# A fourth weight buffer and a fourth PSUM bank in the expert stage of an attention and MoE kernel

## The chip, the cores and the metric

One Trainium2 chip; the program runs on one of its cores. The metric is the device time of one execution in microseconds (us), and lower is better.

## What is computed

Sliding-window attention, then a dense gated layer, then a layer of eight experts of which each token takes one:

```python
# q, k, v: [4, 8, 576, 64]
scores = where((rel >= 0) & (rel < 64), q @ k.T / 8, -1e9)
x = softmax(scores) @ v                     # as [2304, 512]
x = ((x @ w1) * (x @ w2)) @ w3 @ w_out      # [512, 1024] x 2, [1024, 1024], [1024, 512]
e = argmax(x @ w_gate)                      # one of 8 experts for each token
h = maximum(x[mask] @ ew1[e], 0)            # [512, 1024]
out[mask] = gate_w * sigmoid(x @ w_output_gate)[e] * (h @ ew2[e])   # [1024, 512]
```

The weights and tokens are float32. The number of tokens that go to each expert is known only when the program runs.

## The kernel before

Every float32 product is made in three passes (PASSES): each operand is split into a high half in a shorter format and a low half, the rest, and high x high, high x low and low x high are added up in PSUM. A weight therefore needs a split before it is used: ACT copies the high half (ehigh, line 676), DVE subtracts it from the raw chunk (elow, line 680).

Up to about 490 us attention and the dense layer run in an order that a planner writes out. After that comes the expert stage, with which the change deals. Its order is the program's on TensorE alone; on the other engines the framework's scheduler sets the order, and each engine and queue then works strictly in that order.

The expert stage goes through the experts e = 0 to 7. For each:

- static_block takes the first 256 tokens. The first layer makes hidden features in eight groups f of 128: 12 matmuls of 256 columns (line 924) into one PSUM bank, then the eviction by ACT (line 929, relu, the high half) and DVE (line 930, the low half) into hT. The banks come from ps_ab, tag "ab", which has three. The second layer (mm2, line 905) makes two blocks of 128 tokens: for each f three matmuls of 512 columns, which read hT of that f.
- row_block takes the next 128 tokens, if the expert has more than 256, with line 958 for the first layer; a fourth block and a loop for more follow inside branches. Its input xT is made by xT_block: four transposes (line 728), then a split (lines 421 and 422). The third block's tile is exT2 (two buffers), that of the fourth block and of the loop exT3. Its first half accumulates in the bank of ps_v, tag "pv".
- The hooks at1, at2 and at3 of static_block call esplit eight times: they split the weights of expert e + 1, eight chunks of 512 KB each (four of the first layer, four of the second). Chunks are numbered through all experts, 0 to 63; chunks 24 to 31 are expert 3's and are split in expert 2's block. The raw chunks are fetched by SP (eload, lines 662 and 664) into three buffers, tag ck2: after each split the load of the chunk three further on is asked for, and it has to wait until DVE has emptied its buffer.
- The rows of the next experts' tokens come by gathers that POOL issues (line 707) and the results go out by scatters (line 897). All of these share the DMA engines with the weights.

ex[0] is the memory pool of the later part of the stage; it is opened behind expert 0's static block, where the pools of the dense layer are closed, and lies in their memory. Expert 0's own block uses the dense layer's tiles for its hT.

Of the kernel before, what the change touches and what calls it, by code (L numbers as in the profile page):

```python
# [9 lines left out]
F32 = mybir.dt.float32  # L10
F32R = mybir.dt.float32r
# [10 lines left out]
NT, DM, DF, NE = B * S, H * D, 1024, 8  # L22
# [374 lines left out]
def attention_moe_moe_kernel(ctx: ExitStack, tc: tile.TileContext, q0, k0, v, w1, w2, w3, w_out,  # L397
# [4 lines left out]
    def pool(stack, name, **kw):  # L402
        return stack.enter_context(tc.tile_pool(name=name, bufs=kw.pop("bufs", 1), **kw))
# [8 lines left out]
    ps_ab = pool(ctx, "ps_ab", bufs=3, space=PSUM)  # L412
    ps_acc = pool(ctx, "ps_acc", bufs=2, space=PSUM)
    ps_s = pool(ctx, "ps_s", bufs=2, space=PSUM)
    ps_v = pool(ctx, "ps_v", space=PSUM)
# [212 lines left out]


    exp_state = {}  # L630

    def open_exp():
        s_att.close()
        exp_state["p"] = pool(s_exp, "exp", side="right")
# [13 lines left out]
    def eslot(e, i):  # L648
        if ew[e][i] is None:
            j = 0 if e % 2 == 0 else 2 + 2 * i  # L650
            ew[e][i] = [wslot(j), wslot(j + 1)]
        return ew[e][i]

    items = [(e, i, c) for e in range(NE) for i in range(2) for c in range(4)]
    nload, nsplit = [0], [0]

    def eload(to):
        while nload[0] < min(to, len(items)):
            e, i, c = items[nload[0]]
            t = exp_state["p"].tile([128, 1024], F32, name="ck2", tag="ck2", bufs=3)  # L660
            if i == 0:
                nc.sync.dma_start(out=t, in_=ew1[e, 128 * c:128 * c + 128, :])
            else:
                nc.sync.dma_start(out=t.rearrange("p (a d) -> p a d", a=2),
                                  in_=ew2[e, 256 * c:256 * c + 256, :].rearrange("(a p) d -> p a d", p=128))
            eq.append(t)
            nload[0] += 1
# [7 lines left out]
    def ehigh():  # L675
        nc.scalar.activation(out=eparts()[0], in_=eq[0], func=AF.Copy)  # L676

    def elow(low=V):
        hi, lo = eparts()
        low.tensor_tensor(lo, eq.popleft(), hi.bitcast(F32), op=ALU.subtract)  # L680
        nsplit[0] += 1

    def esplit(low=V):
        if nsplit[0] < len(items):
            ehigh()
            elow(low)
            eload(nsplit[0] + 3)

    def step(n=1):
        for _ in range(n):  # L690
# [4 lines left out]
    idx, xg, xTs = {}, {}, {}  # L695
# [35 lines left out]
    def xT_block(g, xT, c0):  # L731
        split(g_turn(g), xT[:, 0, :, c0:c0 + 128], xT[:, 1, :, c0:c0 + 128])
# [153 lines left out]
    post.extend(rt.parts(*GROUPS[NU - 1]))  # L886


    ex = [None]

    def y_tile():
        return ex[0].tile([128, DM], F32, name="y", tag="y", bufs=3)
# [1 line left out]
    def emit_out(ps, ix, j, own=y_tile):  # L894
        y = own()
        nc.scalar.activation(out=y, in_=ps, func=AF.Copy, scale=ix.bitcast(F32)[:, j, 1:2])  # L896
        nc.gpsimd.indirect_dma_start(out=out[:, :],  # L897
                                     out_offset=bass.IndirectOffsetOnAxis(ap=ix[:, j, 0:1], axis=0),
                                     in_=y, in_offset=None, bounds_check=NT - 1, oob_is_err=False)

    def mm2(hT, c0, w, hooks={}):
        ps = ps_acc.tile([128, 512], F32, name="yps", tag="acc")
        for f in range(8):
            for i, (a, b) in enumerate(PASSES):
                mm(ps, lhsT=hT[f][:, a, c0:c0 + 128], rhs=w[b][:, 512 * f:512 * f + 512],  # L905
                   start=f == 0 and i == 0, stop=f == 7 and i == 2)
            if f in hooks:
                hooks[f]()
        return ps

    def h_tile(f):
        return ex[0].tile([128, 2, 256], F32R, name="hT", tag="hT", bufs=8)

    def static_block(e, ix, at1, at2, at3, h_tile=h_tile, y_tile=y_tile):

        w1e = eslot(e, 0)
        xT = xTs.pop(e)
        hT = []
        for f in range(8):
            ps = ps_ab.tile([128, 512], F32, name="hps", tag="ab")  # L920
            for kk in range(4):
                c = 1024 * kk + 128 * f
                for i, (a, b) in enumerate(PASSES):
                    mm(ps[:, 0:256], lhsT=w1e[a][:, c:c + 128], rhs=xT[:, b, kk, :],  # L924
                       start=kk == 0 and i == 0, stop=kk == 3 and i == 2)
                if (f, kk) in at1:
                    at1[f, kk]()
            h = h_tile(f)
            nc.scalar.activation(out=h[:, 0, :], in_=ps[:, 0:256], func=AF.Relu)
            nc.vector.scalar_tensor_tensor(out=h[:, 1, :], in0=ps[:, 0:256], scalar=0.0,  # L930
                                           in1=h[:, 0, :].bitcast(F32), op0=ALU.max, op1=ALU.subtract)
            hT.append(h)
            if f in at1:
                at1[f]()
        w2e = eslot(e, 1)
        for j, at in enumerate((at2, at3)):
            ps = mm2(hT, 128 * j, w2e, at)
            emit_out(ps, ix, j, y_tile)

    def row_block(xT, ix, j, w1e, w2e):  # L940
        hs, hT = [], {}

        def turn(z):
            tp = ps_s.tile([128, 512], F32, name="tps2", tag="S")
            for f in range(4):
                nc.tensor.transpose(tp[:, 128 * f:128 * f + 128], hs[z][:, 128 * f:128 * f + 128], ident)
            tp = tp.rearrange("p (a b) -> p a b", a=4)
            for f in (0, 2):
                h2 = ex[0].tile([128, 2, 2, 128], F32R, name="h2", tag="hT", bufs=8)
                split(tp[:, f:f + 2, :], h2[:, 0], h2[:, 1])  # L950
                hT[4 * z + f], hT[4 * z + f + 1] = h2[:, :, 0, :], h2[:, :, 1, :]

        for z in range(2):
            ps = (ps_s if z else ps_v).tile([128, 512], F32, name="rps", tag="S" if z else "pv")
            for kk in range(4):
                c = 1024 * kk + 512 * z
                for i, (a, b) in enumerate(PASSES):
                    mm(ps, lhsT=xT[:, a, kk, 0:128], rhs=w1e[b][:, c:c + 512],
                       start=kk == 0 and i == 0, stop=kk == 3 and i == 2)
                if z and kk == 1:  # L960
                    turn(0)
            h = ex[0].tile([128, 512], F32, name="hs", tag="y", bufs=3)
            nc.scalar.activation(out=h, in_=ps, func=AF.Relu)
            hs.append(h)
        ps = mm2(hT, 0, w2e, {1: lambda: turn(1)})
        emit_out(ps, ix, j)

    def row_loop(lo, hi, w1e, w2e):

        with tc.For_i(lo, hi, 128) as r:  # L970
            ix = ex[0].tile([128, 1, 2], I32, name="ixd", tag="ixd", bufs=1)
            nc.sync.dma_start(out=ix[:, 0, :], in_=tab[bass.ds(r, 128), :])
            g = ex[0].tile([128, DM], F32, name="xgd", tag="y", bufs=3)
            nc.gpsimd.indirect_dma_start(out=g, out_offset=None, in_=x2d[:, :],
                                         in_offset=bass.IndirectOffsetOnAxis(ap=ix[:, 0, 0:1], axis=0))
            xT = ex[0].tile([128, 2, 4, 128], F32R, name="exT3", tag="exT3", bufs=1)
            xT_block(g, xT, 0)
            row_block(xT, ix, 0, w1e, w2e)

# [42 lines left out]
    w1e, w2e = eslot(0, 0), eslot(0, 1)  # L1022
    n0 = nc.values_load(rt.done[0:1, 0:1], min_val=0, max_val=256)
    n = nc.values_load(rt.cnt[0:1, 0:1], min_val=0, max_val=NT)
    xT = ex[0].tile([128, 2, 4, 128], F32R, name="exT2", tag="exT2", bufs=2)
# [4 lines left out]
    with tc.If(n > n0):  # L1030
        row_block(xT, idx[0], 0, w1e, w2e)
        with tc.If(n > n0 + 128):  # L1032
            row_loop(n0 + 128, n, w1e, w2e)
    for e in range(1, NE):
        at1 = {f: esplit for f in (0, 2, 4, 6)}
        at1[1] = turn
        at3 = {3: esplit, 6: esplit}
        if e + 1 < NE:
            rows(e + 1, tab[e * NT + NT:e * NT + NT + 512, :], 4)
            at3.update({0: lambda e=e: begin(e + 1), 2: turn, 5: turn})  # L1040
        static_block(e, idx[e], at1, {f: esplit for f in (1, 5)}, at3)
        w1e, w2e = eslot(e, 0), eslot(e, 1)
        n = nc.values_load(rt.cnt[0:1, e:e + 1], min_val=0, max_val=NT)  # L1043
        with tc.If(n > 256):  # L1044
            row_block(xTs.pop((e, 2)), idx[e], 2, w1e, w2e)
            with tc.If(n > 384):  # L1046
                xT = ex[0].tile([128, 2, 4, 128], F32R, name="exT3", tag="exT3", bufs=1)
                xT_block(xg[e, 3], xT, 0)
                row_block(xT, idx[e], 3, w1e, w2e)
                with tc.If(n > 512):  # L1050
                    row_loop(e * NT + 512, e * NT + n, w1e, w2e)
    order.close()
    s_ex2.close()
    s_exp.close()
# [46 lines left out]
```

## Time and profile before

| what | value |
|---|---|
| time, median of 3 runs | 799.07 us (795.09 to 799.41) |
| the profiled execution's own time | 800.18 us |
| its span, first to last instruction | 798.5 us |
| TensorE matmuls busy | 741.0 us, 93% of the span |
| DVE, ACT, POOL busy | 378.0, 303.8, 168.4 us |
| moved by DMA | 97.47 MB, mean 122 GB/s |

PE is TensorE, PEld its weight loads, DVE is VectorE, SPq and ACTq the queues of an engine's DMA and branch instructions. In a timeline a row is one instruction or several alike that follow each other: start, time from the first's start to the last's end, engine, line, what is written from what, shape, count, and in brackets how long the engine stood idle before it and what ended that. PEclk is TensorE's granted clock as a share of its full 2.4 GHz; 0.5 is 1.2 GHz. Variables that hold tiles carry the name that the trace gives them: raw chunks are ck, split weights w or wx, the first layer's banks hps, the second's yps.

### The profile page before, as it was taken

The numbers are of one execution on the slowest core, as the hardware profiler recorded it, in microseconds if no ns is written. First come the engines' busy times: TensorE is split into PE (matmuls) and PEld (weight loads), VectorE is DVE, ScalarE is ACT, GpSimd is POOL, SyncE is SP. The second block draws the span as 40 slices with busy tenths as digits, with TensorE's granted clock in tenths as the row PEclk, the third lists the DMA queues.
The fourth block names the chain that finished last, engine by engine and source line by source line (L and its number), as shares of the span: only waits on it lengthen the run. The fifth ranks groups of instructions, "written<-read, shape, count | busy, mean of one in ns | idle before, by whom it ended". The sixth has DMA issues, their size and how long they took to land. (4 is left out here: it accounts for less than half of the span.)

```text
span 798.5 us, 13578 instructions
## 1 busy us (share of the span) xinstructions
PE 741.0 (93%) x5227; PEld 661.0 (83%) x5227; DVE 378.0 (47%) x907; ACT 303.8 (38%) x683; POOL 168.4 (21%) x196
## 2 busy tenths in 40 slices
PE   3799979999999999999999998888989899899995
PEld 2577769989999999999999998868878778788874
DVE  6988995444445344344423226516264552462110
ACT  3554443433334233433221215425254544453221
POOL 6654552110111311110110010050213212010010
PEclk9999998999999999999999999989999999999998
DMA  8946662322222132015000004855456572650010
GB/s 324 409 170 221 208 215 76 122 82 77 98 77 102 33 103 77 8 32 173 27 4 26 28 14 167 185 136 179 126 184 209 187 236 71 228 181 26 6 40 13
DMA packets 38933, 97.47 MB, mean 122 GB/s; under 512 B 9747, under 2 KB 9875, under 8 KB 38848
## 3 DMA queue, kind: packets, MB, share of 16 engines
q1 hardware_dynamic: 33072, 83.06, 31.5%
q0 software_dynamic: 4816, 12.77, 5.1%
q8 instruction: 50, 0.82, 0.4%
q10 hardware_dynamic: 960, 0.53, 0.2%
q14 instruction: 35, 0.29, 0.1%
HBM read 86.83 MB, written 10.65 MB: 122 GB/s over the span
## 5 line engine op out<-in xcount | busy, mean ns | idle before, releaser
L560 PE MATMUL ab<-xt,w 128*128 128x256 f32 x1728 | 229.1, 287 | 0.5 <-DVE f L513 0.5
L560 PEld LDWEIGHTS ab<-xt,w 128*128 128x128 f32 x1728 | 219.1, 193 | 5.2 <-DVE f L513 0.8
L584 PE MATMUL acc<-w,gt 128*128 128x512 f32 x432 | 114.4, 399 | 3.4 <-ACT gt L572 2.6
L584 PEld LDWEIGHTS acc<-w,gt 128*128 128x128 f32 x432 | 76.1, 189 | 17.4 <-ACT gt L572 3.1
L568 DVE TENSOR_TENSOR a_sb<-ab,a_sb 128x256 f32<-128x256 f32 x72 | 30.5, 424 | 121.6 <-PE ab L560 113.2
L905 PE MATMUL yps<-w,hT 128*128 128x512 f32 x336 | 83.9, 401 | 0.0
L177 POOL TENSOR_TENSOR pp<-pp,r 128x384 f32<-128x384 f32 x48 | 39.7, 829 | 191.4 <-DVE r L172 131.5
L680 DVE TENSOR_TENSOR w<-ck,w 128x1024 fp32r<-128x1024 f32 x48 | 58.1, 1221 | 33.9 <-ACT w L676 25.3
L905 PEld LDWEIGHTS yps<-w,hT 128*128 128x128 f32 x336 | 62.4, 192 | 12.1
L572 ACT ACTIVATE gt<-a_sb 128x256 fp32r<-128x256 f32 x72 | 30.0, 416 | 99.8 <-DVE a_sb L568 95.2
L540 PE MATMUL wps<-w,w3T 128*128 128x512 f32 x192 | 52.5, 416 | 11.7 <-ACT w3T L527 11.5
L676 ACT ACTIVATE w<-ck 128x1024 fp32r<-128x1024 f32 x48 | 50.3, 1057 | 32.9 <-DMA ck<-in_moe_w 30.4
L897 POOL DMA_INDIRECT out<-y,idx x20 | 20.1, 1004 | 194.1 <-ACT y L896 139.7
L163 ACT ACTIVATE pp<-sps,nm 128x128 f32<-128x128 f32 x144 | 42.4, 369 | 39.1 <-DVE nm L154 36.8
L924 PE MATMUL hps<-exT,w 128*128 128x256 f32 x384 | 49.1, 286 | 8.0 <-DVE hT L930 6.0
L924 PEld LDWEIGHTS hps<-exT,w 128*128 128x128 f32 x384 | 46.8, 191 | 11.1 <-DVE hT L930 7.3
L540 PEld LDWEIGHTS wps<-w,w3T 128*128 128x128 f32 x192 | 35.4, 195 | 19.3 <-ACT w3T L527 11.5
L565 ACT ACTIVATE a_sb<-ab 128x256 f32<-128x256 f32 x72 | 27.8, 386 | 54.9 <-PE ab L560 51.7
L389 POOL DMA_INDIRECT tab<-ent,pos x18 | 17.7, 982 | 139.2 <-DVE pos L376 42.2
L576 DVE TENSOR_TENSOR gt<-a_sb,gt 128x256 fp32r<-128x256 f32 x72 | 31.3, 435 | 25.4 <-ACT gt L572 24.4
L422 DVE TENSOR_TENSOR exT<-gps,exT 128x512 fp32r<-128x512 f32 x23 | 15.9, 692 | 57.0 <-ACT exT L421 55.5
L924 PE MATMUL hps<-exT,wx 128*128 128x256 f32 x288 | 37.2, 286 | 5.8 <-DVE hT L930 4.3
(132 smaller groups left out, 1035.6 us busy)
## 6 DMA issues: line engine op xcount, KB each, us to landing
ck<-in_moe_w SPq DMA_DIRECT2D x88, 512.0 KB
q<-in_q SPq DMA_DIRECT2D x16, 576.0 KB
v<-in_v SPq DMA_DIRECT2D x16, 576.0 KB
k<-in_k SPq DMA_DIRECT2D x16, 320.0 KB
w<-in_moe_w_out SPq DMA_DIRECT2D x8, 512.0 KB
w<-in_moe_w SPq DMA_DIRECT2D x8, 512.0 KB
x2d<-x SPq DMA_DIRECT2D x16, 256.0 KB
x2d<-x ACTq DMA_DIRECT2D x2, 256.0 KB
```

Source lines behind the costliest of these rows:

```text
L163: nc.scalar.activation(out=p[:, o], in_=ps[:, o], func=AF.Exp, bias=nm[:, i:i + 1], scale=0.125)
L177: nc.gpsimd.tensor_tensor(p, p, s.pop(("r", g)).unsqueeze(2).to_broadcast([128, 3, 128]), op=ALU.mult)
L540: mm(ps, lhsT=t[:, a, 128 * j:128 * j + 128], rhs=wo[b][:, o:o + 512], start=g == 0 and j == 0 and x == 0, stop=g == 1 and j == 3 and x == 2)
L560: mm(ps, lhsT=w[a][:, c:c + 128], rhs=x[:, b, kk, :], start=kk == 0 and i == 0, stop=kk == 3 and i == 2)
L568: V.tensor_tensor(asb[u, m], gps.pop((u, m, 1)), asb[u, m], op=ALU.mult)
L572: nc.scalar.activation(out=g[:, 0, :], in_=asb[u, m], func=AF.Copy)
L576: V.tensor_tensor(g[:, 1, :], asb.pop((u, m)), g[:, 0, :].bitcast(F32), op=ALU.subtract)
L584: mm(accs[u][t], lhsT=g[:, a, 128 * t:128 * t + 128], rhs=ws["w34"][b][:, 512 * m:512 * m + 512], start=m == 0 and i == 0, stop=m == 7 and ...
L676: nc.scalar.activation(out=eparts()[0], in_=eq[0], func=AF.Copy)
L680: low.tensor_tensor(lo, eq.popleft(), hi.bitcast(F32), op=ALU.subtract)
L905: mm(ps, lhsT=hT[f][:, a, c0:c0 + 128], rhs=w[b][:, 512 * f:512 * f + 512], start=f == 0 and i == 0, stop=f == 7 and i == 2)
L924: mm(ps[:, 0:256], lhsT=w1e[a][:, c:c + 128], rhs=xT[:, b, kk, :], start=kk == 0 and i == 0, stop=kk == 3 and i == 2)
```

## The change

Three edits in the expert stage. From the opening of ex[0] on, raw chunks whose number leaves 3 when divided by 4 go to a new buffer, ck3, in that pool, and eload runs four chunks ahead instead of three. In static_block the groups f = 3 and f = 7 take the bank of ps_v, tag "pv", so that four banks go round. The tile exT3 is dropped: the fourth row block and the loop turn their rows into the third block's tile, and row_loop gets it as an argument.

```diff
--- before.py
+++ after.py
@@ -628,6 +628,7 @@
 
 
     exp_state = {}
+    ex = [None]
 
     def open_exp():
         s_att.close()
@@ -657,7 +658,10 @@
     def eload(to):
         while nload[0] < min(to, len(items)):
             e, i, c = items[nload[0]]
-            t = exp_state["p"].tile([128, 1024], F32, name="ck2", tag="ck2", bufs=3)
+            if ex[0] is not None and nload[0] % 4 == 3:
+                t = ex[0].tile([128, 1024], F32, name="ck3", tag="ck3", bufs=1)
+            else:
+                t = exp_state["p"].tile([128, 1024], F32, name="ck2", tag="ck2", bufs=3)
             if i == 0:
                 nc.sync.dma_start(out=t, in_=ew1[e, 128 * c:128 * c + 128, :])
             else:
@@ -684,7 +688,7 @@
         if nsplit[0] < len(items):
             ehigh()
             elow(low)
-            eload(nsplit[0] + 3)
+            eload(nsplit[0] + (3 if ex[0] is None else 4))
 
     def step(n=1):
         for _ in range(n):
@@ -886,7 +890,6 @@
     post.extend(rt.parts(*GROUPS[NU - 1]))
 
 
-    ex = [None]
 
     def y_tile():
         return ex[0].tile([128, DM], F32, name="y", tag="y", bufs=3)
@@ -917,7 +920,7 @@
         xT = xTs.pop(e)
         hT = []
         for f in range(8):
-            ps = ps_ab.tile([128, 512], F32, name="hps", tag="ab")
+            ps = (ps_v if f % 4 == 3 else ps_ab).tile([128, 512], F32, name="hps", tag="pv" if f % 4 == 3 else "ab")
             for kk in range(4):
                 c = 1024 * kk + 128 * f
                 for i, (a, b) in enumerate(PASSES):
@@ -965,7 +968,7 @@
         ps = mm2(hT, 0, w2e, {1: lambda: turn(1)})
         emit_out(ps, ix, j)
 
-    def row_loop(lo, hi, w1e, w2e):
+    def row_loop(lo, hi, w1e, w2e, xT):
 
         with tc.For_i(lo, hi, 128) as r:
             ix = ex[0].tile([128, 1, 2], I32, name="ixd", tag="ixd", bufs=1)
@@ -973,7 +976,6 @@
             g = ex[0].tile([128, DM], F32, name="xgd", tag="y", bufs=3)
             nc.gpsimd.indirect_dma_start(out=g, out_offset=None, in_=x2d[:, :],
                                          in_offset=bass.IndirectOffsetOnAxis(ap=ix[:, 0, 0:1], axis=0))
-            xT = ex[0].tile([128, 2, 4, 128], F32R, name="exT3", tag="exT3", bufs=1)
             xT_block(g, xT, 0)
             row_block(xT, ix, 0, w1e, w2e)
 
@@ -1030,7 +1032,7 @@
     with tc.If(n > n0):
         row_block(xT, idx[0], 0, w1e, w2e)
         with tc.If(n > n0 + 128):
-            row_loop(n0 + 128, n, w1e, w2e)
+            row_loop(n0 + 128, n, w1e, w2e, xT)
     for e in range(1, NE):
         at1 = {f: esplit for f in (0, 2, 4, 6)}
         at1[1] = turn
@@ -1042,13 +1044,13 @@
         w1e, w2e = eslot(e, 0), eslot(e, 1)
         n = nc.values_load(rt.cnt[0:1, e:e + 1], min_val=0, max_val=NT)
         with tc.If(n > 256):
-            row_block(xTs.pop((e, 2)), idx[e], 2, w1e, w2e)
+            xT = xTs.pop((e, 2))
+            row_block(xT, idx[e], 2, w1e, w2e)
             with tc.If(n > 384):
-                xT = ex[0].tile([128, 2, 4, 128], F32R, name="exT3", tag="exT3", bufs=1)
                 xT_block(xg[e, 3], xT, 0)
                 row_block(xT, idx[e], 3, w1e, w2e)
                 with tc.If(n > 512):
-                    row_loop(e * NT + 512, e * NT + n, w1e, w2e)
+                    row_loop(e * NT + 512, e * NT + n, w1e, w2e, xT)
     order.close()
     s_ex2.close()
     s_exp.close()
```

The scheduler also places instructions differently. On ACT, in expert 2's block before, from the second eviction on (L929 are the evictions hT in the order f1, f2 and so on, L676 the splits of chunks 26 to 31):

```order
L676 ACTIVATE w_6848<-ck_6507 128x1024
L929 ACTIVATE hT<-hps 128x256 x2
L676 ACTIVATE w_6848<-ck_6852 128x1024
L929 ACTIVATE hT<-hps 128x256
L676 ACTIVATE w_6985<-ck_6888 128x1024
L929 ACTIVATE hT<-hps 128x256 x2
L676 ACTIVATE w_6985<-ck_6924 128x1024
L929 ACTIVATE hT<-hps 128x256
L676 ACTIVATE w_6985<-ck_6960 128x1024
L929 ACTIVATE hT<-hps 128x256
L676 ACTIVATE w_6985<-ck_6989 128x1024
```

The same place after the change (now L932 and L680):

```order
L680 ACTIVATE w_6847<-ck_6488 128x1024
L932 ACTIVATE hT<-hps 128x256
L680 ACTIVATE w_6847<-ck_6508 128x1024
L932 ACTIVATE hT<-hps 128x256
L680 ACTIVATE w_6984<-ck_6851 128x1024
L932 ACTIVATE hT<-hps 128x256
L680 ACTIVATE w_6984<-ck_6887 128x1024
L932 ACTIVATE hT<-hps 128x256 x2
L680 ACTIVATE w_6984<-ck_6923 128x1024
L932 ACTIVATE hT<-hps 128x256
L680 ACTIVATE w_6984<-ck_6959 128x1024
L932 ACTIVATE hT<-hps 128x256
```

Both begin with chunk 26's split. Before, f3 stands behind the split of chunk 27, f4 and f5 behind 28, f6 behind 29 and f7 behind 30; after, f3 stands behind 28, f4 and f5 behind 29, f6 behind 30 and f7 behind 31. DVE's order follows, with the splits of 27 and 28 next to each other ahead of f3.

On SP, at the branch into expert 0's row blocks (L1030 before), the piece before that holds the first chunk load behind the branch, chunk 19:

```order
L970 UNCONDITIONAL_BRANCH
L1032 UNCONDITIONAL_BRANCH
L1030 UNCONDITIONAL_BRANCH
L662 DMA ck_6283<-in_moe_w 128x1024
L664 DMA ck_6326<-in_moe_w 128x2x512
```

After, with the same branch now at L1032:

```order
L1045 TENSOR_LOAD cnt
L1045 ISA x2
L666 DMA ck_6282<-in_moe_w 128x1024
L1032 COMPARE_AND_BRANCH
L1034 REGISTER_ALU
L1034 COMPARE_AND_BRANCH
```

Chunk 19's load, the first into ck3, has moved from behind the branch to ahead of it. In each later block one load has moved in the same way, from the start of the next expert's block to the end of this one's. TensorE's and POOL's orders are unchanged.

## Rows read from the trace of the kernel before

**Rows 1.** The page, part 1: busy us (share of the span) and instructions.
```profile
PE 741.0 (93%) x5227; PEld 661.0 (83%) x5227; DVE 378.0 (47%) x907; ACT 303.8 (38%) x683; POOL 168.4 (21%) x196
```

**Rows 2.** Windows of the first layers, experts 2 to 7: stretch, length, engines, PEclk, DMA, GB/s.
```profile
580.59:594.76 14.17, 12.30 (x97) 11.76 (x97) 9.21 (x13) 9.44 (x15) 2.34 (x2) 1.00 0.52 176
607.36:622.26 14.90, 12.35 (x97) 11.74 (x97) 9.21 (x13) 9.56 (x15) 2.53 (x2) 1.00 0.61 196
634.86:649.12 14.26, 12.36 (x96) 11.75 (x97) 9.21 (x13) 9.30 (x15) 2.74 (x2) 1.00 0.65 211
673.84:688.30 14.46, 12.31 (x97) 11.77 (x97) 9.20 (x13) 9.42 (x15) 1.98 (x2) 1.00 0.58 187
703.05:715.78 12.73, 11.99 (x96) 11.69 (x97) 9.20 (x13) 8.43 (x15) 1.02 (x1) 1.00 0.66 198
740.50:752.27 11.77, 11.76 (x96) 11.67 (x97) 2.97 (x7) 3.04 (x8) 0.98 (x1) 1.00 0.02 6
```

**Rows 3.** Timeline of TensorE, expert 1's first layer: start, length, what [idle before <-releaser].
```profile
554.34 1.69 PE L924 MATMUL hps<-exT,w 128*128 128x256 f32 x12 [1.38 <-DVE hT L930]
```

**Rows 4.** Waits, 480 us to the end: who, for whom: us in total, times, longest.
```profile
PE hps L924 <- DVE hT L930: 10.4, 9, 2.3
...
PE gps L728 <- DMA xg<-x2d,idx: 2.6, 3, 1.2
```

**Rows 5.** Timeline of TensorE, expert 2's block.
```profile
580.59 10.90 PE L924 MATMUL hps<-exT,wx 128*128 128x256 f32 x84 [0.43 <-PEq L1046]
593.22 1.70 PE L924 MATMUL hps<-exT,wx 128*128 128x256 f32 x12 [1.73 <-DVE hT L930]
594.76 6.31 PE L905 MATMUL yps<-w,hT 128*128 128x512 f32 x27
```

**Rows 6.** Timeline of ACT, expert 2's block.
```profile
587.10 1.06 ACT L676 ACTIVATE w<-ck 128x1024 fp32r<-128x1024 f32 x1 [1.51 <-DMA ck<-in_moe_w]
...
590.52 1.06 ACT L676 ACTIVATE w<-ck 128x1024 fp32r<-128x1024 f32 x1 [2.09 <-DMA ck<-in_moe_w]
...
593.62 1.06 ACT L676 ACTIVATE w<-ck 128x1024 fp32r<-128x1024 f32 x1 [0.28 <-DMA ck<-in_moe_w]
```

**Rows 7.** Timeline of DVE, expert 2's block.
```profile
588.19 1.23 DVE L680 TENSOR_TENSOR w<-ck,w 128x1024 fp32r<-128x1024 f32 x1 [1.34 <-ACT w L676]
589.33 0.42 DVE L930 SCALAR_TENSOR_TENSOR hT<-hps,hT 128x256 fp32r<-128x256 f32 x1
591.61 1.23 DVE L680 TENSOR_TENSOR w<-ck,w 128x1024 fp32r<-128x1024 f32 x1 [1.86 <-ACT w L676]
592.75 0.75 DVE L930 SCALAR_TENSOR_TENSOR hT<-hps,hT 128x256 fp32r<-128x256 f32 x2
```

**Rows 8.** Timeline of SP: the first chunk loads in the blocks of experts 1 and 2.
```profile
544.71 0.34 SPq L662 DMA_DIRECT2D ck<-in_moe_w  x1
...
583.60 0.33 SPq L662 DMA_DIRECT2D ck<-in_moe_w  x1
584.74 8.49 SPq L664 DMA_DIRECT2D ck<-in_moe_w  x4
```

**Rows 9.** Windows, columns as in rows 2: expert 2's loads, expert 0's gathers.
```profile
584.00:593.00 9.00, 7.35 (x58) 6.81 (x56) 5.79 (x9) 4.95 (x10) 1.34 (x1) 1.00 0.77 262
522.00:527.00 5.00, 2.40 (x12) 1.75 (x12) 1.13 (x2) 1.88 (x3) 3.22 (x4) 0.75 0.64 177
```

**Rows 10.** Windows, columns as in rows 2: the matmuls after expert 5's first layer.
```profile
688.30:696.22 7.92, 7.92 (x31) 6.32 (x30) 2.90 (x4) 2.09 (x3) 0.00 (x0) 0.78 0.74 249
```

**Rows 11.** Timeline of TensorE: expert 0's second layer, and the first transposes behind it.
```profile
510.97 11.07 PE L905 MATMUL yps<-w,xt 128*128 128x512 f32 x48
522.97 0.66 PE L728 MATMUL gps<-ident,xg 128*128 128x128 f32 x4 [0.93 <-DMA xg<-x2d,idx]
```

**Rows 12.** Timeline of TensorE: the transposes of expert 7's fourth block.
```profile
774.98 0.60 PE L728 MATMUL gps<-ident,xg 128*128 128x128 f32 x4
```

## The prediction

> **What bounds the kernel now.** I read the page first: TensorE is busy 741.0 of the 798.5 us [rows 1]. So time can come off only where TensorE has nothing to do, and the change touches the expert stage alone. There I cut out, with the windows view, each expert's first layer, from its first matmul of line 924 to its first of line 905 [rows 2]. Expert 7 splits no weights any more and takes 11.77 us: the price of the 96 matmuls alone, 1.47 us for each of the eight f. Experts 2 to 6 do the same in 14.17, 14.90, 14.26, 14.46 and 12.73 us, which is 2.40, 3.13, 2.49, 2.69 and 0.96 more. Expert 1 has four transposes among them, so I take the wait that its row shows, 1.38 [rows 3]. Together the six blocks lose **13.0 us**. The waits view names who ends most of it: DVE's eviction of hT, nine times, 10.4 us [rows 4].
>
> Why the eviction is late shows in expert 2's block, which starts at 580.59 [rows 5 to 8]. ACT and DVE work in order, and the evictions of f (lines 929, 930) stand between the splits of expert 3's chunks 24 to 31 (lines 676, 680). Three chunks are there at the start. Chunk 27 can be fetched only when DVE has emptied chunk 24's buffer: issued at 583.60, split by ACT at 587.10. Chunk 28, issued at 584.74, is split at 590.52, after ACT stood 2.09 us waiting for the DMA [rows 6, 8]. Behind it wait f4 and f5, and DVE is done with f4 at about 592.75 + 0.37 = 593.12 [rows 7]. With three banks f7 needs f4's, so TensorE starts it at 593.22 [rows 5], instead of 580.59 + 7 x 1.47 = 590.88.
>
> **The change, part by part.**
>
> *The bank.* f7 now needs f3's bank, not f4's. In expert 2's block f3 is free at 589.33 + 0.42 = 589.75 [rows 7], before 590.88: no stall is left. The second layer then starts at 580.59 + 11.77 = 592.36 and takes 0.70 us per f (27 matmuls, nine f, 6.31 us [rows 5]), so it wants f4 at 595.2 and f7 at 597.3; f4 is there at 593.1. The new bank, pv, is otherwise taken by the row blocks, which come after the block; nobody waits for it.
>
> *The fourth buffer.* It brings one chunk more into the idle stretch, but the built order uses that up: on ACT f3 now stands behind chunk 28, f4 and f5 behind 29, f7 behind 31. In expert 2's block chunk 28 goes out when chunk 24 is done, at 583.60, as chunk 27 did, and if it lands as that did, f3 is free at 589.75 and f4 at 593.1, both as before. DVE takes 27 and 28 before f3, but 27 is there from the start and is over before 28 comes. Chunk 31 is asked for after 27's split, not after 28's, which ended at 592.84 [rows 7]; if it lands by 593.62, when ACT could split chunk 30 before [rows 6], f7 is done at 593.62 + 1.06 + 1.23 + 0.42 = 596.3, before 597.3. So by this chain the bank carries the gain, and the buffer leaves four chunks to land inside the block instead of five. I count the **13.0 us** whole. The unknown is how long chunk 28 takes: 3.5 us from issue to split (583.60 to 587.10) or 5.8 (584.74 to 590.52) [rows 6, 8]. It is the first load after an idle stretch, as chunk 27 was, so I take 3.5 and keep 5.8 for the range.
>
> *The clock.* After expert 5's stall the 27 matmuls that follow took 7.92 us at a granted clock of 0.78 [rows 10], after expert 2's the same took 6.31 [rows 5]. Without the stall I expect 6.31 there: **1.6 us** off. Only one of the stalls was followed by a fall, so this term is 0 to 1.6.
>
> *The first load into the new buffer.* The order moves chunk 19's load from behind expert 0's branch to before it. Its memory was that of expert 0's last hT tiles, so it goes out when expert 0's second layer ends, at 510.97 + 11.07 = 522.04 [rows 11], and not at 544.71 [rows 8]. There it meets the gathers of line 707, for which TensorE waits three times, 2.6 us in all [rows 4, 11]. SP has only branches behind the load, so nothing is queued there. The loss is bounded by nothing, if the gathers keep their turn, and by 2.0 us, if they wait for all of it: 0.52 MB at the 262 GB/s of a busy stretch [rows 9]. The DMA is 0.64 busy in these 5 us, which leaves 0.36 x 5 = 1.8 us for the load, but not where it likes; I take the middle, **1.0 us** lost. The Trainium skill says (DMA: Bandwidth & Descriptors, section Queues, rings and completion order) that each DMA engine takes turns, packet by packet, between the queues that have work. By that the last of the three gathers would meet the whole load and come 2.0 us late, and the sum would be 787.6; no row here shows these gathers beside a load.
>
> *The rest.* Later row blocks now write into the third one's xT. Only expert 7 ran a fourth block here, and its transposes, at 774.98 [rows 12], stand on TensorE behind all the third block's matmuls: nothing is left to wait for. The new buffer is as large as the tile that goes, 4 KB a partition. Expert 0's block also gets the bank; its waits are for other things, so I count nothing.
>
> Sum, against the profiled execution's own 800.18 us: 800.18 - 13.0 - 1.6 + 1.0 = 786.6. That execution stands 1.1 us over the median of 799.07, less than the clock's term alone; I forecast **786.5 us**.
>
> **The rivals.**
>
> *The loads stay late.* If chunk 28 takes 5.8 us, it lands at 589.4; ACT and DVE then need 1.06 + 1.23 + 0.42, some 0.1 of it overlapped, until f3 is free at 592.0, and f7 starts 1.1 us late: about half of expert 2's 2.40 stays. Over six blocks 6.5 us are won and the clock's term is lost: 800.2 - 6.5 + 1.0 = 794.7. For it speaks that the DMA is 0.77 busy there [rows 9]; against it, the 3.5 us at the same place in the queue. Chance 0.15.
>
> *The bank does nothing.* Then only the buffer acts, and by the chain above f3 and f4 come free when they did: 800.2 + 1.0 = 801.2, which can't be told from no change. Against it: the row that ends the stall is f4's eviction, and f3's is 3.4 us earlier [rows 7]. Chance 0.07. A sentence of the Trainium skill reads that way, of a kernel whose matmuls wait for DMA: "Adding PSUM double-buffering gave no further gain" (TensorE: Matmul & The Clock Gate, section HAM oscillation). By it the sum would be 801.2 as well; the trace agrees that a DMA stands at the root, but shows a bank between it and TensorE.
>
> *Slower: the evictions behind one more split.* f3 was behind chunk 27 and is now behind 28. If 28 lands late enough, f7 starts later than before. To lose 4.0 us in all, with 1.0 from the gathers, the six blocks must lose 13.0 + 3.0 = 16.0, or 2.7 each: f3 free at 593.6, so chunk 28 landing at 591.0, 7.4 us after its issue, in every block. That gives 804.2. It decides from 6.9 us on, where f3 would come free when f4 did; the longer of the two rows is 5.8. Chance 0.03.
>
> **How the numbers follow.** A measurement of this kernel can tell about 0.5%, 4.0 us, from no change. The forecast has 0.75, with a range of its own of 783.5 to 789: the load costing 0 to 2.0, the clock giving 0 to 1.6, and the median's 1.1 under the profiled execution. To it come 0.15 for 794.7 (still faster, by just over 0.5%), 0.07 and 0.03. So faster 0.90, same 0.07, slower 0.03. The range runs from 783.5 to 795.0, through the second case, and leaves the last two out.
>
> **What would show it.** In the profile after, the windows of rows 2 should read 11.8 to 12.2 us for experts 2 to 6; TensorE's wait for DVE's hT should fall from 10.4 to under 2 us; ACT should still wait for chunks between f2 and f6; chunk 19's load should be issued near 522, and the waits for gathers grow from 2.6 to some 3.6 us. If the windows stay at 14, the bank is not the limit; if they read 13, chunk 28 lands late, and its issue and split tell by how much.

## The result, and the profile after

The changed kernel takes **785.77 us** (median of six executions, five of them from 785.29 to 786.65), against 798.97 us (795.09 to 803.88) for the kernel before on the same chip. The sixth execution took 1152.04 us, at a mean granted clock of 0.653 where the others had 0.981 to 0.985, and is left out of the ratio. The ratio is 0.984, with a 95% interval of 0.982 to 0.987: faster by 1.6%. The forecast was 786.5 us. The profiled execution took 785.67 us, 14.5 less than that of before.

The first part of the page, as in [rows 1], says that TensorE is busy 94% of the span, after 93%:

```profile
PE 734.4 (94%) x5227; PEld 658.0 (84%) x5227; DVE 377.2 (48%) x907; ACT 302.0 (39%) x683; POOL 168.1 (21%) x196
```

The windows of the first layers of experts 2 to 7, cut as in [rows 2] (stretch, length, busy time and count of PE, PEld, DVE, ACT, POOL, then PEclk, DMA share, GB/s):

```profile
580.20:591.81 11.61, 11.61 (x97) 11.61 (x97) 8.98 (x12) 7.99 (x13) 2.34 (x2) 1.00 0.61 217
604.41:615.99 11.58, 11.58 (x97) 11.58 (x97) 9.42 (x13) 9.56 (x15) 2.52 (x2) 1.00 0.78 259
628.59:640.23 11.64, 11.64 (x96) 11.62 (x97) 7.73 (x10) 8.22 (x13) 2.74 (x2) 1.00 0.73 241
664.95:676.56 11.61, 11.61 (x96) 11.61 (x97) 8.98 (x12) 8.08 (x14) 1.98 (x2) 1.00 0.68 228
689.84:701.43 11.59, 11.59 (x97) 11.59 (x97) 9.24 (x13) 8.98 (x14) 1.02 (x1) 1.00 0.65 212
726.14:737.83 11.69, 11.69 (x96) 11.67 (x97) 2.97 (x7) 3.03 (x8) 0.98 (x1) 1.00 0.02 7
```

Length and TensorE's busy time are now the same number in every row. Experts 2 to 6, which lost 0.96 to 3.13 us each, are as fast as expert 7, which has no splits at all. The waits view, in the stretch of [rows 4], has no row for DVE's hT any more; its first row, and ACT's row for chunks, are these:

```profile
PE gps L732 <- DMA xg<-x2d,idx: 4.6, 2, 2.9
...
ACT w L680 <- DMA ck<-in_moe_w: 24.4, 21, 2.1
```

So ACT still stands 24.4 us for the loads; TensorE no longer notices. How that can be is in expert 2's block. TensorE, as in [rows 5]:

```profile
580.20 11.77 PE L927 MATMUL hps<-exT,wx 128*128 128x256 f32 x96 [0.43 <-PEq L1049]
591.81 6.31 PE L908 MATMUL yps<-w,hT 128*128 128x512 f32 x27
```

ACT, as in [rows 6], with the splits of chunks 28 and 30:

```profile
587.16 1.06 ACT L680 ACTIVATE w<-ck 128x1024 fp32r<-128x1024 f32 x1 [1.58 <-DMA ck<-in_moe_w]
...
592.09 1.06 ACT L680 ACTIVATE w<-ck 128x1024 fp32r<-128x1024 f32 x1 [1.98 <-DMA ck<-in_moe_w]
```

DVE, as in [rows 7], with the evictions of f3, of f4 and f5, of f6 and of f7:

```profile
589.39 0.42 DVE L933 SCALAR_TENSOR_TENSOR hT<-hps,hT 128x256 fp32r<-128x256 f32 x1
...
590.86 0.75 DVE L933 SCALAR_TENSOR_TENSOR hT<-hps,hT 128x256 fp32r<-128x256 f32 x2
...
594.33 0.42 DVE L933 SCALAR_TENSOR_TENSOR hT<-hps,hT 128x256 fp32r<-128x256 f32 x1
...
595.79 0.42 DVE L933 SCALAR_TENSOR_TENSOR hT<-hps,hT 128x256 fp32r<-128x256 f32 x1
```

SP's queue, as in [rows 8]: chunk 19, and chunks 28 and later:

```profile
522.65 0.34 SPq L666 DMA_DIRECT2D ck<-in_moe_w  x1
...
583.21 4.80 SPq L668 DMA_DIRECT2D ck<-in_moe_w  x4
```

The eight f take 11.61 us, 1.45 each, so f7 wants f3's bank at 580.20 + 7 x 1.45 = 590.35; f3 is free at 589.39 + 0.42 = 589.81, half a microsecond before. The second layer wants f7 of hT at 591.81 + 7 x 0.70 = 596.7; DVE ends it at 595.79 + 0.42 = 596.2. Both margins are thin, and in this block both hold.

**Where the 14.5 us are.** From one expert's first matmul to the next one's, out of [rows 2, 3, 5] and the starts above (expert 1 starts at 542.23 before, 543.46 after):

| from the start of expert | before | after | gained | predicted: stall, clock |
|---|---|---|---|---|
| 1 | 38.36 | 36.74 | 1.62 | 1.38 |
| 2 | 26.77 | 24.21 | 2.56 | 2.40 |
| 3 | 27.50 | 24.18 | 3.32 | 3.13 |
| 4 | 38.98 | 36.36 | 2.62 | 2.49 |
| 5 | 29.21 | 24.89 | 4.32 | 2.69 + 1.6 |
| 6 | 37.45 | 36.30 | 1.15 | 0.96 |
| 1 to 6 | 198.27 | 182.68 | 15.59 | 14.6 |

Each block gains its stall (expert 5's also the clock's term) and between 0.03 and 0.24 us more, mostly since a first layer without a wait takes 11.6 and not the 11.77 that was taken from expert 7. Before expert 1's start 1.23 us are lost, behind expert 7's start 0.14 won: 15.59 - 1.23 + 0.14 = 14.5, the whole of it.

What is lost shows at expert 0's row block. TensorE, as in [rows 11]:

```profile
524.02 0.66 PE L732 MATMUL gps<-ident,xg 128*128 128x128 f32 x4 [1.73 <-DMA xg<-x2d,idx]
527.57 1.85 PE L732 MATMUL gps<-ident,xg 128*128 128x128 f32 x8 [2.90 <-DMA xg<-x2d,idx]
529.07 5.45 PE L961 MATMUL rps<-wx,exT 128*128 128x512 f32 x18
```

and POOL's timeline, with the issue of the first three gathers, in whose midst chunk 19's load goes out:

```profile
520.71 0.98 POOL L711 DMA_INDIRECT xg<-x2d,idx  x1 [12.50 <-issue]
522.55 0.96 POOL L711 DMA_INDIRECT xg<-x2d,idx  x1 [0.86 <-issue]
523.82 0.95 POOL L711 DMA_INDIRECT xg<-x2d,idx  x1 [0.30 <-issue]
```

The waits for gathers grew by 2.0 us (2.6 to 4.6), twice what was forecast. But the first gather was itself issued 1.05 us later than before (520.71 against 519.66), which the load at 522.65 cannot have done. The second and the third go out 1.22 us later (522.55 against 521.33, 523.82 against 522.60), the second of them ahead of the load, and that is the whole of the 1.23 us: from the third to expert 1's start both kernels take the same, 19.64 us and 19.63 before. The row block's first matmul does come 0.70 us later behind that gather (5.25 us against 4.55), but its first 18 matmuls then take 5.45 us at a granted clock of 0.78, where they took 6.31 at 0.67, and make up for it. So other runs had to say what the load costs.

### The profile page after: what moved, and what is told of

Read it like the earlier page. It is cut to its first block, busy times and chain, and to the rows that moved or that the text cites. A ratio compares the mean times of both kernels' runs of the same rounds, so it can differ in the third digit from the quotient of the medians.

```text
span 784.0 us, 13573 instructions
## 1 busy us (share of the span) xinstructions
PE 734.4 (94%) x5227; PEld 658.0 (84%) x5227; DVE 377.2 (48%) x907; ACT 302.0 (39%) x683; POOL 168.1 (21%) x196
## 5 line engine op out<-in xcount | busy, mean ns | idle before, releaser
L908 PE MATMUL yps<-w,hT 128*128 128x512 f32 x336 | 82.3, 395 | 0.0
L908 PEld LDWEIGHTS yps<-w,hT 128*128 128x128 f32 x336 | 61.3, 188 | 11.6
L540 PE MATMUL wps<-w,w3T 128*128 128x512 f32 x192 | 52.7, 417 | 11.7 <-ACT w3T L527 11.6
L680 ACT ACTIVATE w<-ck 128x1024 fp32r<-128x1024 f32 x48 | 50.3, 1057 | 27.0 <-DMA ck<-in_moe_w 24.4
L540 PEld LDWEIGHTS wps<-w,w3T 128*128 128x128 f32 x192 | 35.5, 196 | 19.4 <-ACT w3T L527 11.6
L927 PE MATMUL hps<-exT,w 128*128 128x256 f32 x384 | 47.4, 284 | 1.9 <-PEq L1049 0.9
L389 POOL DMA_INDIRECT tab<-ent,pos x18 | 17.6, 980 | 139.5 <-DVE pos L376 42.2
L576 DVE TENSOR_TENSOR gt<-a_sb,gt 128x256 fp32r<-128x256 f32 x72 | 31.3, 434 | 25.4 <-ACT gt L572 24.4
L145 PE MATMUL sps<-k,q 128*128 128x128 f32 x288 | 41.4, 282 | 1.0 <-DMA k<-in_k 1.0
```

The costliest lines, as they stand in the source:

```text
L145: nc.tensor.matmul(ps[:, 128 * i:128 * i + 128], lhsT=s["q"][:, 128 * c:128 * c + 128], rhs=s["k"][:, 64 * c:64 * c + 128], start=False, s ...
L540: mm(ps, lhsT=t[:, a, 128 * j:128 * j + 128], rhs=wo[b][:, o:o + 512], start=g == 0 and j == 0 and x == 0, stop=g == 1 and j == 3 and x == 2)
L576: V.tensor_tensor(g[:, 1, :], asb.pop((u, m)), g[:, 0, :].bitcast(F32), op=ALU.subtract)
```

## The experiments

Each ratio is to runs of the kernel before on the same chip. Two theories gave nearly the same total for the changed kernel: that the **bank** carries the gain, and that the **buffer** does, by bringing the splits forward. Runs 1, 2, 4 and 5 shared a chip and 17 executions of the kernel before (median 798.11 us).

**1. The bank alone**, on the kernel before:

```diff
-            ps = ps_ab.tile([128, 512], F32, name="hps", tag="ab")
+            ps = (ps_v if f % 4 == 3 else ps_ab).tile([128, 512], F32, name="hps", tag="pv" if f % 4 == 3 else "ab")
```

> The kernel before with the fourth bank alone: f = 3 and f = 7 in pv, three raw buffers, exT3 as before. Theory A (the bank carries the gain): first layers of experts 1 to 6 at 11.8 to 12.1 us, ACT still waiting some 30 us for chunks, waits for the gathers near 522 back at 2.6 us, so about 785 us, a little below the changed kernel's 785.8. Theory B (the earlier loads carry it): first layers at 14 us, about 799. Theory C (each does a part): 12.5 to 13.5 us, 790 to 794.

Measured: 784.73 us (781.42 to 788.72), ratio 0.985 [0.982, 0.988]. TensorE has no row of waits for hT. Expert 2's block, on ACT (the splits of chunks 27 and 28):

```profile
581.77 1.06 ACT L676 ACTIVATE w<-ck 128x1024 fp32r<-128x1024 f32 x1 [1.51 <-DMA ck<-in_moe_w]
...
584.99 1.06 ACT L676 ACTIVATE w<-ck 128x1024 fp32r<-128x1024 f32 x1 [1.89 <-DMA ck<-in_moe_w]
```

on DVE (f4 and f5):

```profile
587.22 0.75 DVE L930 SCALAR_TENSOR_TENSOR hT<-hps,hT 128x256 fp32r<-128x256 f32 x2
```

and on TensorE:

```profile
575.27 11.77 PE L924 MATMUL hps<-exT,wx 128*128 128x256 f32 x96 [0.43 <-PEq L1046]
586.88 6.31 PE L905 MATMUL yps<-w,hT 128*128 128x512 f32 x27
```

The order is that of before, and the loads are as late: ACT's waits for chunks, in the stretch of [rows 4], before and with the bank alone, are

```profile
ACT w L676 <- DMA ck<-in_moe_w: 30.4, 24, 2.7
...
ACT w L676 <- DMA ck<-in_moe_w: 31.5, 22, 2.5
```

f4 starts its eviction 587.22 - 575.27 = 11.95 us into the block, within 0.2 us of the 592.75 - 580.59 = 12.16 of [rows 5, 7]. Yet f7 doesn't wait, as it needs f3's bank; the second layer wants f4 only at 586.88 + 4 x 0.70 = 589.7. The stretch from expert 1's start to expert 7's is 183.16 us, against 182.68 in the changed kernel and 198.27 before. One bank takes the evictions' lateness off the path, though they come as late as before.

**2. The buffer alone**, the changed kernel with three banks:

```diff
-            ps = (ps_v if f % 4 == 3 else ps_ab).tile([128, 512], F32, name="hps", tag="pv" if f % 4 == 3 else "ab")
+            ps = ps_ab.tile([128, 512], F32, name="hps", tag="ab")
```

> The changed kernel with its hidden groups back in the three banks of ps_ab: the fourth buffer and the shared xT alone. Theory A: f6 and f7 still wait for the evictions of f3 and f4, first layers at 14 us, and chunk 19's early load costs the gathers 1 to 2 us: 799 to 801 us. Theory B: first layers at 12 us, about 786. Theory C: 12.5 to 13.5 us, 790 to 794.

Measured: 793.42 us (12 runs, 788.70 to 797.79), ratio 0.993 [0.991, 0.996]. It gains about 5 us, where by the prediction's chain it should gain nothing. TensorE in the blocks of experts 1, 2 and 3 (its profiled execution is its slowest, 797.79 us):

```profile
546.15 8.87 PE L927 MATMUL hps<-exT,w 128*128 128x256 f32 x72
...
579.57 9.09 PE L927 MATMUL hps<-exT,wx 128*128 128x256 f32 x72 [0.43 <-PEq L1049]
588.92 1.69 PE L927 MATMUL hps<-exT,wx 128*128 128x256 f32 x12 [0.26 <-DVE hT L933]
592.23 1.70 PE L927 MATMUL hps<-exT,wx 128*128 128x256 f32 x12 [1.63 <-DVE hT L933]
...
619.37 2.37 PE L927 MATMUL hps<-exT,w 128*128 128x256 f32 x12 [1.73 <-DVE hT L933]
621.53 7.25 PE L908 MATMUL yps<-w,hT 128*128 128x512 f32 x27
```

In expert 2's block the chain held to the number: f7 starts 592.23 - 579.57 = 12.66 us in, as the 593.22 - 580.59 = 12.63 of [rows 5]. In expert 1's the stall is gone: chunk 19, on the chip early, no longer stands in the row of loads there, which is the likely reason. The window of the second layer behind expert 3's stall shows the fall of the clock that [rows 10] had shown behind expert 5's:

```profile
621.53:628.78 7.25, 7.25 (x30) 5.88 (x30) 1.09 (x2) 1.02 (x2) 0.00 (x0) 0.86 0.49 163
```

**3. The same kernel once more**, on another chip, one execution, to see whether these stalls are fixed.

> A second profile of the fourth buffer alone, whose runs went from 788.7 to 797.8 and whose profiled one was the slowest. If the buffer shortens some blocks for good (experts 1, 5 and 6 in the first profile) and the rest was a fall of the clock in expert 3's block: the same blocks again short, 14 us in experts 2 to 4, no clock fall, 790 to 794 us. If it was chance: other blocks short.

Measured: 793.76 us, one execution. They are fixed only in part. TensorE in expert 2's block:

```profile
581.76 9.09 PE L927 MATMUL hps<-exT,wx 128*128 128x256 f32 x72 [0.43 <-PEq L1049]
591.30 3.17 PE L927 MATMUL hps<-exT,wx 128*128 128x256 f32 x24 [0.45 <-DVE hT L933]
```

f7 no longer waits here, where it waited 1.63 us in run 2. TensorE's waits for hT sum to 3.5 us here and to 7.4 in run 2's profile, against 10.4 before. The first layers of experts 1 and 6 have no wait in either profile, as the expectation for a gain that stays had it; those of experts 2, 3 and 5 are shorter here than in run 2, and expert 4's is not. In expert 2's block ACT waited 1.98 us for chunk 29's load in run 2 and not at all in run 3. With three banks and four buffers most stalls hang on when a load lands, and that varies from execution to execution.

**4. The load of chunk 19 put back** behind the branch, in the changed kernel:

```diff
-            if ex[0] is not None and nload[0] % 4 == 3:
+            if nload[0] > 20 and nload[0] % 4 == 3:
...
-            eload(nsplit[0] + (3 if ex[0] is None else 4))
+            eload(nsplit[0] + (3 if nsplit[0] < 20 else 4))
```

> The changed kernel, but the fourth buffer and the run-ahead of four begin only with chunk 23, so that chunk 19 is loaded behind the branch again, near 544. If its early load is what makes the gathers late: TensorE's waits for gathers fall from 4.6 to about 2.6 us, expert 1's first layer starts 0.5 to 1.5 us earlier, about 784.8 us. If the later start of expert 1 has another cause: as the changed kernel, 785.8.

Measured: 784.41 us (783.43 to 786.46), ratio 0.984 [0.981, 0.986]. As an experiment on the load it failed: the scheduler put chunk 23's load, now the first into the new buffer, in the same place. SP's queue:

```profile
522.24 0.37 SPq L668 DMA_DIRECT2D ck<-in_moe_w  x1
```

**5. The changed kernel again**, beside these three:

> The changed kernel itself on the same chip as the other three, to compare them with: 785.5 to 786.5 us, first layers at 11.8 us.

Measured: 783.97 us (781.03 to 786.40), ratio 0.983 [0.981, 0.986]. Beside the 784.73 us of the bank alone, on the same chip, no effect of the buffer can be told apart.

**What the early load costs.** The kernels of these runs let it be measured all the same, by a stretch that begins after the first gather's own lateness: from the issue of the third gather to the first matmul of expert 0's row block (L958 or L961).

| kernel | load beside the gathers | us |
|---|---|---|
| before | no | 527.15 - 522.60 = 4.55 |
| bank alone | no | 524.82 - 520.48 = 4.34 |
| bank from expert 1 on (run 8) | no | 527.93 - 523.34 = 4.59 |
| shared xT alone (run 7) | no | 531.02 - 526.74 = 4.28 |
| after | yes | 529.07 - 523.82 = 5.25 |
| after, again | yes | 524.03 - 518.72 = 5.31 |
| buffer alone, runs 2 and 3 | yes | 5.08, 5.23 |
| chunk 19 put back | yes (chunk 23) | 527.53 - 522.15 = 5.38 |

The means are 4.4 and 5.25, and no profile with the load is as short here as one without: one load of 0.52 MB delays the first matmul behind these gathers by about **0.8 us**. Up to expert 1's first matmul the same kernels differ by 1.0 us in the mean (18.8 and 19.8), but those without the load alone spread from 18.05 to 19.63. The Trainium skill says that each DMA engine takes turns between its queues, packet by packet (DMA: Bandwidth & Descriptors, section Queues, rings and completion order); the prediction's reading of it, by which the last gather would meet the whole load, made the delay 2.0, and the runs show less than half.

**6. The bank with fewer buffers.** If loads don't matter once the bank is there, two raw buffers should do on the kernel before:

```diff
-            t = exp_state["p"].tile([128, 1024], F32, name="ck2", tag="ck2", bufs=3)
+            t = exp_state["p"].tile([128, 1024], F32, name="ck2", tag="ck2", bufs=2)
...
-            eload(nsplit[0] + 3)
+            eload(nsplit[0] + 2)
...
-            ps = ps_ab.tile([128, 512], F32, name="hps", tag="ab")
+            ps = (ps_v if f % 4 == 3 else ps_ab).tile([128, 512], F32, name="hps", tag="pv" if f % 4 == 3 else "ab")
```

> The kernel before with the fourth bank, and with two raw buffers instead of three (eload two ahead). If the bank is what cuts TensorE loose from the loads, f7 needs only f3, which now stands behind chunk 26, the first to be fetched in the block: first layers of experts 2 to 6 at 11.8 to 12.5 us, ACT's wait for chunks well over 35 us, about 785 to 788 us (expert 0's block may lose up to 3 us, since its own chunks have two buffers as well). If the number of loads in the block counts whatever the banks, first layers at 13 to 15 us and 793 to 800.

Measured: 800.39 us (797.05 to 803.98), against 800.14 for the kernel before: ratio 1.000 [0.998, 1.003]. No gain is left, though TensorE's waits for hT sum to only 0.3 us. The time is lost in other places. TensorE at a turn of expert 1's, in expert 3's first layer, and at expert 6's start:

```profile
567.86 0.66 PE L728 MATMUL gps<-ident,xg 128*128 128x128 f32 x4 [1.30 <-DVE exT L422]
...
610.32 11.95 PE L924 MATMUL hps<-exT,w 128*128 128x256 f32 x86 [2.41 <-issue]
...
699.83 13.07 PE L924 MATMUL hps<-exT,wx 128*128 128x256 f32 x96 [3.34 <-PEq L1044]
```

The first is a wait for DVE's split of xT, which stands behind a chunk's split on ACT and DVE. The row at 610.32 names "issue": the profile shows nothing that TensorE waited for. These are the last split of a chunk for expert 3, on DVE, and the split on ACT that ends just before 610.32:

```profile
604.69 1.23 DVE L680 TENSOR_TENSOR w<-ck,w 128x1024 fp32r<-128x1024 f32 x1 [0.84 <-ACT w L676]
...
609.07 1.06 ACT L676 ACTIVATE wx<-ck 128x1024 fp32r<-128x1024 f32 x1 [2.11 <-DMA ck<-in_moe_w]
```

Expert 3's weights were thus complete at 605.92, before its first layer began at 606.38. ACT's split ends at 610.13, but it writes wx, the first layer of an expert with an even number, here expert 4, and so cannot be what TensorE needed. A gap stands behind the same ten matmuls in runs 9 and 10 (1.97 and 1.94 us), with the bank and without it, and there TensorE goes on more than 1 us after ACT's split is over. In all three the DMA view has one packet of the kind "instruction" in flight just before TensorE stops, at 607.7, 612.9 (run 9) and 609.8 us (run 10); whether the gap is a wait for code is not shown. Each of the two long waits is followed by a fall of the clock, as the windows behind them show:

```profile
610.32:622.11 11.79, 11.79 (x86) 11.79 (x86) 6.99 (x11) 5.63 (x11) 1.27 (x2) 0.86 0.66 185
699.83:712.74 12.91, 12.91 (x97) 12.91 (x98) 7.51 (x11) 7.14 (x12) 0.12 (x1) 0.88 0.55 153
```

The second of these stretches, expert 6's first layer, took 12.91 us for what takes 11.6 at full clock. From expert 1's start to expert 7's this kernel takes 193.54 us, 10.9 more than the changed one: 2.4 and 2.5 in the long waits (of the 3.34, 0.83 is there after the change as well), 1.4 and 1.3 by the clock behind them, 1.3 at the turn, and 2.0 in smaller pieces, most of them in expert 4's block. Ahead of expert 1 two loads stand beside the gathers instead of one, and the stretch of the table above takes 8.7 us, 2.6 of it a wait of the transposes for a split of xT. So the bank takes the waits for hT away here too, but other waits stand in their place. Only the turn's is traced back to late chunks; what TensorE waits for in expert 3's first layer, and what holds it and ACT at the branch until 699.8, the profile doesn't say, and both stay open.

**7. The shared xT alone**, the changed kernel with three banks and three buffers:

```diff
-            if ex[0] is not None and nload[0] % 4 == 3:
+            if False:
...
-            eload(nsplit[0] + (3 if ex[0] is None else 4))
+            eload(nsplit[0] + 3)
...
-            ps = (ps_v if f % 4 == 3 else ps_ab).tile([128, 512], F32, name="hps", tag="pv" if f % 4 == 3 else "ab")
+            ps = ps_ab.tile([128, 512], F32, name="hps", tag="ab")
```

> The kernel before with exT3 dropped and the third block's tile used for later row blocks, three buffers and three banks. Expected by every theory: nothing to wait for, 797 to 799.5 us, the 0.88 us ahead of expert 7's fourth block as before, first layers as in the kernel before. If the shared tile made a wait, its place would be at the fourth block, and it could be up to the 5 us that a row block's first layer takes.

Measured: 799.73 us against 800.14, ratio 0.999 [0.996, 1.002]. Expert 7's fourth block waits 0.88 us for its split, as it does in the kernel before and after the change:

```profile
776.58 4.67 PE L961 MATMUL rps<-w,exT 128*128 128x512 f32 x18 [0.88 <-ACT exT L421]
```

**8. The bank from expert 1 on.** In the changed kernel a small wait had come up in expert 0's block (0.42 us, for DVE's xt of line 933, at 496.01). On the kernel before, the bank was given to experts 1 to 7 alone:

```diff
-            ps = ps_ab.tile([128, 512], F32, name="hps", tag="ab")
+            ps = (ps_v if e and f % 4 == 3 else ps_ab).tile([128, 512], F32, name="hps", tag="pv" if e and f % 4 == 3 else "ab")
```

> The fourth bank alone, but only from expert 1 on. If expert 0's block loses by the bank (the changed kernel has a new wait of 0.42 us there, since its logits use the same three banks): 0.2 to 0.6 us less than the bank alone, 784.2 beside its 784.7, too little for these rounds to tell, but the 0.42 us wait should be gone from the trace. If not: the wait stays.

Measured: 787.93 us (785.95 to 790.50), ratio 0.985 [0.981, 0.990]. A wait of the same kind stands a few matmuls later, though expert 0's block has no fourth bank here:

```profile
498.73 1.34 PE L924 MATMUL hps<-xt,wx 128*128 128x256 f32 x9 [0.56 <-DVE xt L930]
```

Other profiles say more: with the bank in expert 0's block, runs 1 and 5 have no such wait, and run 7, without the bank, has the same 0.4 us at the same place. So it comes and goes with the execution and not with the bank. The stretch from expert 1 to 7 is 183.23 us, as with the bank in all blocks.

**9 and 10. Two buffers without the bank, and with it.** Run 6 doesn't say what the bank gives in its setting. So the kernel before with two buffers and nothing else (the first two pieces of run 6's edit) ran beside the kernel of run 6, on one chip:

> The kernel before with two raw buffers and three banks, nothing else. With two buffers and the bank the time was 800.4 us, as before's. If with two buffers only the late operands bind (splits slipping behind the first layer), the bank gives nothing there, and this kernel takes 799 to 803 us as well. If the bank gives in this setting what it gives with three buffers (13 us and more, as the evictions are then later still), this kernel takes 812 to 822 us, with waits of TensorE for hT of 13 us or more, and stays that much above the next one.

> Two raw buffers and the bank, again beside the kernel with two buffers alone on the same chip: 798 to 803 us, TensorE's waits for hT under 1 us. The difference of the two is what the bank gives when loads are later.

Measured: 801.80 us without the bank (10 runs, 798.05 to 808.69), ratio 1.004 [1.000, 1.007]; 800.43 with it (10 runs, 797.15 to 804.96), ratio 1.003 [1.000, 1.006]. The intervals overlap: with two buffers the bank gives nothing that can be measured, where with three it gave 13 us. The waits view of TensorE (who, for whom: us in total, times, longest) of the expert stage without the bank:

```profile
PE hps L924 <- DVE hT L930: 9.5, 5, 3.7
PE gps L728 <- DMA xg<-x2d,idx: 6.9, 2, 6.0
PE hps L924 <- issue: 2.1, 2, 2.0
```

and with it:

```profile
PE gps L728 <- DMA xg<-x2d,idx: 5.9, 2, 4.2
PE hps L924 <- PEq L1044: 4.1, 2, 4.0
PE gps L728 <- DVE exT L422: 3.9, 2, 2.7
PE hps L924 <- DVE hT L930: 2.2, 1, 2.2
PE hps L924 <- issue: 1.9, 1, 1.9
```

In these two executions (808.69 and 802.12 us, the one without the bank its slowest) the bank takes 7.3 us of waits for hT away, and most comes back elsewhere: 4.1 instead of 0.7 us at the branch of line 1044 (4.0 of it ahead of expert 6), and 3.9 instead of 1.1 for the splits of xT, which stand on ACT and DVE among the splits of late chunks. The theory that the bank would give its 13 us here too is out.

No version beat both kernels: the bank alone and the whole change can't be told apart.

## Why the prediction was right, and where it was not

*The bank.* The term was 13.0 us; the six blocks gave back 15.6 with the clock, and the bank alone gives the same stretch to 0.5 us. The mechanism is the one argued from expert 2's chain, f7 behind f3's eviction instead of f4's. It is shown: run 1 leaves f4 as late as it was and the stall is gone. The windows read 11.6 us for experts 2 to 6, just under the 11.8 to 12.2 that the prediction named. The rival "the bank does nothing" falls with it. The Trainium skill's sentence "Adding PSUM double-buffering gave no further gain" (TensorE: Matmul & The Clock Gate, section HAM oscillation) is about another kernel, already reordered so that TensorE stays warm, and does not carry over. Here the DMA stays the root, 31.5 us of ACT's waits, and one bank gives 1.5%: TensorE's waits were for evictions that stood behind the late load, and those can be buffered. With two buffers (runs 9 and 10) the bank gives nothing that can be measured; why is only in part known, as the profile names no cause for the two longest waits of run 6 behind expert 1's start.

*The chunk behind the idle stretch.* The prediction took 3.5 us from chunk 28's issue to its split and kept 5.8. It was 587.16 - 583.21 = 3.95, so f3 came free 0.5 us before it was wanted. The rival "the loads stay late", worked out with 5.8, did not occur; by the margin, another 0.6 us would have begun to cost in this block.

*The clock.* The term of 1.6 us was right for the profiled execution: behind expert 5's first layer the 27 matmuls take 6.31 us, and that expert's row of the table shows 4.32 = 2.69 + 1.6. What the prediction called uncertain stays so for the kernel before: the clock falls behind some stalls only, and in run 7's profile, which has all the stalls, behind none of the first layers. The changed kernel shows none behind a first layer.

*The first load into the new buffer.* The term was 1.0 us, between 0 and 2.0; the runs give 0.8 at the row block's first matmul. That the profiled execution lost 1.23 us ahead of expert 1, close to the term, was luck: its gathers were issued 1.22 us later, and what the load cost behind them came back by the clock. The issue at 522.65 was forecast at 522.04. The sign that the prediction named, waits for gathers of "some 3.6 us", was a bad one: they read 4.6 here and 2.3 to 6.9 over the other kernels (4.3 in run 7, without the load), as the first gather's issue wanders.

*The buffer alone.* Here a step failed: "by this chain the bank carries the gain, and the buffer leaves four chunks to land inside the block instead of five", with "f3 and f4 come free when they did" for all six blocks. It had been worked out for expert 2's block and was true there in one profile, not in the other. The blocks of experts 1 and 6 have no stall in either, and in others the loads land earlier in some executions. The buffer alone is worth 0.7%, not nothing. This didn't touch the total, because the two gains overlap: 1.5% for the bank, 0.7% for the buffer, 1.6% for both.

*The rest.* Shared xT, nothing: run 7 shows it to about 0.3%. Expert 0's block, nothing: the wait of 0.42 us that came up there comes and goes with the execution, with the bank and without it (runs 1, 5, 7 and 8).

The forecast came within 0.7 us by two small errors that cancel in part: a first layer takes 11.6 and not 11.77 us, which gave 1.0 more, and 1.23 us instead of 1.0 were lost ahead of expert 1, by gathers that were late already when the load went out. The interval of the ratio alone spans 4 us, so a hit to 0.7 us is in part luck; what is shown is the size of the bank's term.

## What to carry to other kernels

When a matmul waits for an eviction, follow the eviction back along its own engine: if it only stands behind work that waits for a DMA, another PSUM bank can hide the lateness without a faster load. Then look at which consumer is the next to feel that lateness, here the second layer and, with two buffers, the transposes that wait for xT's split, and compare its due time with what is left. A chain worked out in one block shouldn't be multiplied by six before the loads' times have been read in the others.

## What the runs showed of the hardware

- The clock falls behind some waits of TensorE and not behind others of the same length. A wait of 1.73 us in expert 2's block before left the next 27 matmuls at 6.31 us [rows 5]; one of 1.73 us in expert 3's block with the buffer alone was followed by 2.37 us for 12 matmuls, 7.25 for 27, at a granted clock of 0.86. The two waits of run 6 (2.41 and 3.34 us) were both followed by falls, but of two waits at the same place as the first, one of 1.97 us in run 9 was followed by a fall (86 matmuls in 12.27 us, granted clock 0.86) and one of 1.94 us in run 10 was not (86 in 10.64 us, granted clock 1.00).
- The issue of the first of expert 0's last gathers, late in its second layer, wanders by several microseconds whatever the variant: 16.8 us behind the router's matmul L356 before, 17.6 after, 15.5 in run 5, the same kernel, and from 14.7 to 19.2 over all kernels. It may be a good part of the scatter between executions, which is not shown, and it is why small effects in that block had to be measured from a later start.
- A load of 0.52 MB that goes out among gathers of another queue puts off the first matmul behind them by 0.8 us (4.4 to 5.25 us over nine profiles), less than half of its own 2.0 us at the 262 GB/s of [rows 9].
